# Out weights widened beside group 1, input weights during part 1's later stages, and four more raw buffers

## The chip, the cores and the metric

The kernel runs on one core of a Trainium2 chip. Its time is the device time of one execution, in microseconds (us). Three executions of the kernel before gave 655.83, 656.95 and 657.58, median 656.95.

## The reference, cut to what matters

```python
# attention over 2 x 8 heads, 768 positions, 64 columns a head: each query sees the keys less than
# 16 positions away, and one summary (maximum of keys, mean of values) per block of 32 keys
x = attention.transpose(0, 2, 1, 3).reshape(1536, 512)
xn = x / sqrt(mean(x * x) + 1e-6) * rms_g
g = xn @ w_gate; val = xn @ w_val                  # 512 x 1536 each       part 1
x = (g / (1 + exp(-g)) * val) @ w_out              # 1536 x 512
h = x @ w_in                                       # 512 x 2048            part 2
out = ((h - tanh(h)) @ w_out2)                     # 2048 x 512
```

The weights arrive as 64-bit floats. The result is float32.

## The kernel before, in words

**Numbers.** A float32 product is made of three matmuls (helper `mm3`, L807 to L809): each operand is split into a rounded high part and the rest, and high x high, low x high and high x low are added up. The high part is a ScalarE copy, the low part a subtraction on VectorE or GpSimd. A 64-bit weight must first become a float32: 128 x 512 of them are loaded as 512 KB into a raw buffer of 128 x 1024 words, ScalarE scales the upper words (L766, or L1278 for an out weight of part 2), VectorE shifts them (L767, L1279) and merges bits of the lower words (L768, L1280). The code calls this to widen. There are two raw buffers (pool `raw`), and a chain keeps their loads in one order on SyncE's queue.

**Stages.** Tokens go in three groups of four tiles of 128. Group 0's attention comes first. Beside its product with part 1's weights (`step`: w_gate and w_val in 12 blocks of 128 columns, then w_out) the attention of groups 1 and 2 runs (`one_unit`, 16 of the 24 units; the text calls this stage "beside group 1"). Then groups 1 and 2 go through part 1 together in six "wide" pairs of blocks (`combine`, `wide_pair`), with seven products instead of eight of sums and differences of sub-blocks; `combine` makes seven operands, each a high and a low part, of the tokens. Group 1's sum over w_out is made there. Group 2's is made in twelve late steps (`late_step`), one per block, 12 matmuls of 512 columns each: they read h from the weights' old places, round it (L825) and take the rest (L828). Part 2 then takes each group through eight pairs of blocks (`pair`), again with seven products per pair (42 matmuls of 256 columns) and 24 matmuls of 512 for the out weight; partial products are kept and added by L1425, L1444 and L1418, and L1479 and L1480 split the result.

**Part 2's weights.** For group 0 the input weights are widened (`widen_second`, 16 of them, one 512 KB load each), combined and split (`make`), and stored to DRAM tensors `ki`; groups 1 and 2 fetch them from there. Out weights are widened and split beforehand (`make_out`, 16 of them), stored as a high and a low half (`ko`, L1289), and fetched when used (L1257).

**Order.** The whole program is a list of operations with engine, estimated duration, dependences, buffers and a due time; `Plan.order` sorts it into one fixed order per engine before the program is built. Each engine then runs its order strictly, and an operation that waits holds up all behind it on its engine. A due time thus sets a place in the order. All DMAs stand on SyncE's queue.

**Places.** `hi_r`, `lo_r`, `wd_r`, `pad` and `rest` are regions of the on-chip memory which the stages use in turn. `pad` is the attention's workspace, `wd` holds part 1's weights, `hi_r[1]` and `hi_r[2]` are the high parts' places of groups 1 and 2. Before, `combine` put the operands 1 and 2 into `hi_r[1]` and `hi_r[2]`, and 6, 7, 5, 3 into `pad`, which is free after the last attention unit. `make_out` used places in `wd` that are free once the input weights of blocks 1 and 3 have been used (`gv_ops[1] + gv_ops[3]`), so all out weights came after group 0's steps.

## Time and profile before

| | us |
|---|---|
| median of three executions | 656.95 |
| profiled execution | 654.7 |
| its span, first to last instruction | 652.9 |
| TensorE busy | 634.8 |
| VectorE busy | 468.6 |
| ScalarE busy | 371.2 |
| GpSimd busy | 81.0 |

The page has the busy time of each engine, the span in 40 slices, the DMA queues, the chain of work that ended last, and the costliest groups of instructions. PE is TensorE, DVE VectorE, ACT ScalarE, POOL GpSimd, SP SyncE. Times in a timeline are from the start of the span. Matmuls overlap in the records (0.39 us each for 512 columns), so their rate is read from their starts. The stages in the span: group 0's attention to about 55 us, group 0's part 1 beside the other groups' attention to 197, the wide pairs to 350, the late steps to 385, part 2 to the end, with group 0 until 471.

### The profile page before, as it was taken

How to read it: one execution, taken by the hardware profiler on the slowest of the kernel's cores; microseconds unless marked ns; L12 is line 12 of the kernel's file. 1: busy time of each engine (PE TensorE's matmuls, PEld its weight loads, DVE VectorE, ACT ScalarE, POOL GpSimd, SP SyncE). 2: the span in 40 equal slices, each digit the busy share in tenths (PEclk: the TensorE clock that was granted, in tenths of full speed). 3: DMA queues.
4: the chain of work that ended last, by engine and by line, in shares of the span. 5: the costliest groups of instructions: out<-in, count | busy, mean ns of one | idle time of the engine just before them, and what ended most of it. 6: DMA issues, size and time to landing. Idle time of an engine off the chain costs nothing.

```text
span 652.9 us, 10519 instructions
## 1 busy us (share of the span) xinstructions
PE 634.8 (97%) x3642; PEld 542.3 (83%) x3642; DVE 468.6 (72%) x1037; ACT 371.2 (57%) x782; POOL 81.0 (12%) x142
## 2 busy tenths in 40 slices
PE   7999999999999999999999999989999999999996
PEld 6998888897888888888787878879989899888985
DVE  5789868886689799989988969986663343433333
ACT  3996676887665566666658747644553232433322
POOL 2213232131123024011200000010000000000000
PEclk9999999999999999999999999989999999999998
DMA  9987556555400023434452588977899787898742
GB/s 341 345 279 274 159 179 209 161 154 181 143 1 0 1 77 133 147 129 130 161 150 92 212 288 266 347 282 281 320 318 357 255 307 246 282 332 298 258 170 97
DMA packets 52254, 136.54 MB, mean 209 GB/s; under 512 B 6200, under 2 KB 8680, under 8 KB 52200
## 3 DMA queue, kind: packets, MB, share of 16 engines
q1 hardware_dynamic: 52200, 135.86, 61.1%
q8 instruction: 29, 0.48, 0.3%
q14 instruction: 25, 0.20, 0.1%
HBM read 109.62 MB, written 26.21 MB: 208 GB/s over the span
## 4 chain that ended last, share of the span: by engine, by line
PE 79%; DMA 10%; DVE 6%; ACT 3%; issue 1%; SPq 0%; POOL 0%; ACTq 0%; DVEq 0%; POOLq 0%
PE bank L809 14%; PE bank L807 14%; PE bank L808 14%; PE mid L807 10%; PE mid L809 9%; PE mid L808 9%; DMA raw<-in_w_dram 5%; PE bank L655 2%; PE bank L561 2%; DMA pad<-in_units_dram 2%; PE bank L666 1%; PE bank L612 1%; DMA out_dram<-th 1%; DMA wd<-in_ksum_dram 1%; DMA wd<-in_units_dram 1%
## 5 line engine op out<-in xcount | busy, mean ns | idle before, releaser
L809 PE MATMUL bank<-oh,hl 128*128 128x512 f32 x192 | 76.7, 399 | 0.9 <-DVE hl L1480 0.9
L807 PE MATMUL bank<-oh,hh 128*128 128x512 f32 x192 | 76.3, 398 | 0.1
L808 PE MATMUL bank<-ol,hh 128*128 128x512 f32 x192 | 75.5, 393 | 0.0
L1463 ACT ACTIVATE lo<-lo 128x512 f32<-128x512 f32 (+1 forms) x48 | 25.2, 524 | 57.4 <-DVE lo L1418 57.4
L807 PE MATMUL mid<-hi,ih 128*128 128x512 f32 (+1 forms) x136 | 54.0, 397 | 0.0
L807 PE MATMUL bank<-hh,oh 128*128 128x512 f32 (+1 forms) x128 | 50.2, 392 | 0.1
L809 PE MATMUL mid<-hi,il 128*128 128x512 f32 (+1 forms) x136 | 50.1, 368 | 0.0
L808 PE MATMUL bank<-hl,oh 128*128 128x512 f32 (+1 forms) x128 | 48.7, 380 | 1.0 <-DVE hl L828 0.8
L809 PE MATMUL bank<-hh,ol 128*128 128x512 f32 (+1 forms) x128 | 48.4, 378 | 0.0
L807 PE MATMUL mid<-pad,ih 128*128 128x512 f32 (+1 forms) x128 | 44.6, 349 | 2.1 <-ACT up L1425 1.9
L809 PEld LDWEIGHTS bank<-oh,hl 128*128 128x128 f32 x192 | 36.3, 189 | 10.5 <-DVE hl L1480 2.0
L1480 DVE TENSOR_TENSOR hl<-lo,hh 128x512 fp32r<-128x512 f32 x48 | 31.5, 687 | 18.2 <-ACT hh L1479 18.1
L808 PE MATMUL mid<-pad,ih 128*128 128x512 f32 (+1 forms) x128 | 44.4, 346 | 0.0
L809 PE MATMUL mid<-pad,il 128*128 128x512 f32 (+1 forms) x128 | 44.3, 346 | 0.0
L766 ACT ACTIVATE wd<-raw 128x512 f32<-128x512 f32 x46 | 31.0, 674 | 22.4 <-DMA raw<-in_w_dram 22.2
L1467 DVE TENSOR_TENSOR lo<-lo 128x512 f32<-128x512 f32 (+1 forms) x48 | 27.1, 565 | 22.9 <-ACT lo L1463 22.7
L808 PE MATMUL mid<-lo,ih 128*128 128x512 f32 (+1 forms) x112 | 40.6, 362 | 0.0
L807 PEld LDWEIGHTS bank<-oh,hh 128*128 128x128 f32 x192 | 36.4, 190 | 4.4 <-ACT hh L1479 0.3
L808 PEld LDWEIGHTS bank<-ol,hh 128*128 128x128 f32 x192 | 36.4, 190 | 4.5
L589 ACT ACTIVATE pad<-pad,st 128x184 f32<-128x184 f32 x88 | 32.3, 439 | 7.0 <-DVE st L575 7.0
L1418 DVE TENSOR_TENSOR lo<-up,bank 128x256 f32<-128x256 f32 x25 | 10.5, 419 | 36.0 <-PE bank L809 35.7
L1074 ACT COPY lo<-mid 128x512 f32<-128x512 f32 x36 | 21.1, 586 | 19.5 <-PE mid L809 19.1
(235 smaller groups left out, 1826.9 us busy)
## 6 DMA issues: line engine op xcount, KB each, us to landing
raw<-in_w_dram SPq DMA_DIRECT2D x62, 512.0 KB, 4.0
wd<-ki SPq DMA_DIRECT2D x32, 512.0 KB, 5.5
oh<-ko SPq DMA_DIRECT2D x48, 256.0 KB, 4.0
ol<-ko SPq DMA_DIRECT2D x48, 256.0 KB, 4.7
wd<-ki SPq DMA_DIRECT2D x32, 384.0 KB, 6.3
pad<-in_units_dram SPq DMA_DIRECT2D x19, 442.0 KB, 4.4
ko<-wd SPq DMA_DIRECT2D x32, 256.0 KB, 2.6
ki<-ih SPq DMA_DIRECT2D x7, 512.0 KB, 4.7
```

The costliest lines, as they stand in the source:

```text
L561: nc.tensor.matmul(ps[e][:, j * SC:(j + 1) * SC], q[r, j], k[r, j], start=(j == 0), stop=(j == NP - 1), skip_group_check=True,)
L589: nc.scalar.activation(s, s, AF.Exp, bias=st[:, 0, h:h + 1], scale=-1.0)
L655: nc.tensor.matmul(av[:, h * (D + 1):(h + 1) * (D + 1)], ph[:, h * P:(h + 1) * P], v[:, h], start=(h == 0), stop=False, skip_group_check=True,
L766: a = act(0.58, lambda d=d, w=w: nc.scalar.activation(d, w(k=1).bitcast(F32), AF.Prelu, scale=2.0 ** -112, alpha=-(2.0 ** 32)), ld, *after ...
L807: nc.tensor.matmul(o, ah, bh, start=first, stop=False, skip_group_check=True)
L808: nc.tensor.matmul(o, ah, bl, start=False, stop=False, skip_group_check=True)
L809: nc.tensor.matmul(o, al, bh, start=False, stop=last, skip_group_check=True)
L1074: o = act(0.52, lambda: nc.scalar.copy(u[m][:], mx[m][:]), *after, *wide_first, slots=[u[m], mx[m]])
L1418: return dve(0.38, lambda: nc.vector.tensor_tensor(out(), x(), z(), ALU.add), *after, slots=slots)
L1463: o = act(us, lambda: nc.scalar.activation(out(), x(), AF.Tanh), *after, slots=slots)
L1467: return dve(us, lambda: nc.vector.tensor_tensor(out(), x(), z(), ALU.subtract), *after, slots=slots)
L1480: l = dve(0.62, lambda j=j: nc.vector.tensor_tensor(hl[j][:], th[j][:], r32(hh[j][:]), ALU.subtract), h, slots=[th[j], hh[j], hl[j]], port ...
```

## The change

Six of the sixteen out weights (`SOON`) are now widened beside group 1, each with a due time before the end of that stage. Their results lie in `hi_r[1]` (pool `oq`, two places). For that `combine` has other homes: operands 1, 2, 6 and 7 in `pad`, 5 in `hi_r[2]`, 3 in `hi_r[1]`. The attention units of groups 1 and 2 are due 8 us sooner (`DONE`). The widening of part 1's weights from block 4 on, and the six out weights, alternate between the old raw buffers and two new ones in `hi_r[2]` (`rawt`); later every third load goes to one place in `wd` (`rawl`). The other ten out weights take turns in the list with the input weights, which go to other places (`AREA`: each pair of blocks of part 2 has its 1024 columns where a block of part 1's weights has been used up), and are made in one buffer (`op`) instead of three. `make_out` needs no separate place for the float32 value. A program that was built from each file gives the orders below. In the changed file L764 is L776, L766 is L778, L1276 is L1292, L1289 is L1306, L825 is L838, L783 is L796, L837 is L850, L1365 is L1381, L1425 is L1440, L1444 is L1459, L1463 is L1478 and L1479 is L1494.

```diff
 OPS = 7
 AHEAD = 20.0
+SOON = 6
 SLACK = 2.0
 BACK = 8
-DONE = 20.0
+DONE = 28.0
 LAND = 1.0
 FAR = 4.0
 GROWS = (slice(32, 64), slice(64, GROW + 2 * NB))
...
         h, f = divmod(f, NF1 // 2)
         return wd[h][:, f * W1:(f + 1) * W1]
+    AREA = 3, 7, 9, 11, 1, 6, 8, 10
+
     def w_second(f):
-        a = at_second(f)
-        return wd[1][:, a:a + 512]
-
-    def at_second(f):
-        n, e = divmod(f, 2)
-        if n < 6:
-            return ((2 * n + 1) if n < 3 else 2 * (n - 3)) * W1 + e * 512
-        return (2 * (n - 6) + e) * W1 + cut1
+        return area(f // 2)[:, f % 2 * 512:(f % 2 + 1) * 512]
+
+    def area(n):
+        h, a = divmod(AREA[n], NF1 // 2)
+        return wd[h][:, a * W1:a * W1 + 1024]
     def h_place(f):
         h, a = divmod(f, NF1 // 2)
...
     cut1 = 2 * NC_ * P
     chain = {}
-
-
+    as_u32 = lambda t: lambda: t().bitcast(U32)
+    plan.pools["rawt"] = Buffers([as_u32(hi_r[2].part(i * 1024, (i + 1) * 1024, F32)) for i in range(2)])
+    plan.pools["rawl"] = Buffers([wd[0][:, 5 * W1:5 * W1 + 1024].bitcast(U32)])
+    plan.pools["oq"] = Buffers([hi_r[1].part(i * 1024, (i + 1) * 1024, F32) for i in range(2)])
+    rawt_ops = []
+    rawl_ops = []
+    turn_raw = [0, 0]
+
+    def raw_slot(early):
+
+        turn_raw[early] += 1
+        n = turn_raw[early]
+        if early:
+            return (slot("rawt"), [], rawt_ops) if n % 2 else (slot("raw"), [], [])
+        return (slot("rawl"), gv_ops[5], rawl_ops) if not n % 3 else (slot("raw"), [], [])
     def widen(nm, src, dst, n, *after):
         done = []
...
                 raw = fixed(early_raw[i].bitcast(U32))
                 free = ksum_op[0] if i < 3 else vsum_op[0][0] + vsum_op[0][1]
             else:
-                raw = slot("raw")
-                free = []
+                raw, free, users = (slot("raw"), [], []) if nm in ("a0", "a1", "a2", "a3") else raw_slot(nm[0] == "a")
             d = dst[:, o:o + 512]
             du = d.bitcast(U32)
             w = lambda raw=raw, k=0: raw[:].rearrange("p (n k) -> p n k", k=2)[:, :, k]
...
     def combine(due):
         k2 = 1024
-        home = {1: (hi_r[1], 0), 2: (hi_r[2], 0), 4: (hi_r[0], 0)}
-        for i, n in enumerate((6, 7, 5, 3)):
+        home = {4: (hi_r[0], 0), 5: (hi_r[2], 0), 3: (hi_r[1], 0)}
+        for i, n in enumerate((1, 2, 6, 7)):
             home[n] = (pad, 2 * k2 * i)
         base = {(k, l): (lo_r[1 + l], k * k2) for k in range(2) for l in range(2)}
         base["t"] = (rest, 0)
...
         def split_sum(n, b, after, slots=()):
             r, a = home[n]
-            free = unit_ops if r is pad else first_ops if r is hi_r[0] else []
+            free = unit_ops if r is pad else {4: first_ops, 5: rawt_ops, 3: made_o}[n]
             by = due + 2 * MM * 2 * (1, 2, 6, 7, 5, 3, 4).index(n)
             out = []
             for c in range(2):
...
     for i, tag in enumerate(("lh", "ll")):
         plan.pools[tag] = Buffers([wd_r[0].part(k * 1024, (k + 1) * 1024, F32R) for k in range(i, 8, 2)])
     plan.pools["tb"] = Buffers([lo_r[0].part(i * 512, (i + 1) * 512, F32) for i in range(NC_)])
-    plan.pools["tq"] = Buffers([lo_r[2].part(i * 512, (i + 1) * 512, F32) for i in range(4)] + [lo_r[1].part(i * 512, (i + 1) * 512, F32) for i in range(2)])
+    plan.pools["tq"] = Buffers([lo_r[1].part(i * 512, (i + 1) * 512, F32) for i in range(2)] + [lo_r[2].part(i * 512, (i + 1) * 512, F32) for i in range(4)])
     plan.pools["sq"] = Buffers([rest.part(0, 1024, F32), lo_r[1].part(1024, 2048, F32)])
-    plan.pools["os"] = Buffers([wd[0][:, 3 * W1 + i * 512:3 * W1 + (i + 1) * 512] for i in range(2)])
-    plan.pools["op"] = Buffers([wd[0][:, W1:W1 + 1024]])
+    plan.pools["op"] = Buffers([area(4)])
     operand = {}
     ready = {}
     prepared = {}
...
     def make_out(f, due):
         n, j = divmod(f, 2)
-        raw, d, o = slot("raw"), slot("os"), slot("op")
+        early = f < SOON
+        raw, free, users = raw_slot(early)
+        o = slot("oq" if early else "op")
         w = lambda k: raw[:].rearrange("p (n k) -> p n k", k=2)[:, :, k]
-        du = lambda: d[:].bitcast(U32)
+        d = lambda: o[:, 512:]
+        du = lambda: d().bitcast(U32)
         src = w2[f].bitcast(U32)
-        gate = gv_ops[1] + gv_ops[3]
-        ld = dma(0.524, lambda: nc.sync.dma_start(raw[:], src[:, 1024:2048]), chain.get("raw"), slots=[raw], land=FAR)
+        gate = [] if early else gv_ops[1]
+        ld = dma(0.524, lambda: nc.sync.dma_start(raw[:], src[:, 1024:2048]), chain.get("raw"), *free, slots=[raw], land=FAR)
         chain["raw"] = ld
-        a = act(0.58, lambda: nc.scalar.activation(d[:], w(1).bitcast(F32), AF.Prelu, scale=2.0 ** -112, alpha=-(2.0 ** 32)), ld, *gate, slots=[raw, d])
-        a = dve(0.34, lambda: nc.vector.tensor_scalar(du(), du(), 3, None, ALU.logical_shift_left), a, slots=[d], port=True)
-        a = dve(0.6, lambda: nc.vector.scalar_tensor_tensor(du(), w(0), 29, du(), ALU.logical_shift_right, ALU.bitwise_or), a, slots=[raw, d], port=True)
-        a = act(0.52, lambda: nc.scalar.copy(o[:, :512].bitcast(F32R), d[:]), a, chain.get("op"), *gate, slots=[d, o])
+        a = act(0.58, lambda: nc.scalar.activation(d(), w(1).bitcast(F32), AF.Prelu, scale=2.0 ** -112, alpha=-(2.0 ** 32)), ld, *gate, slots=[raw, o])
+        a = dve(0.34, lambda: nc.vector.tensor_scalar(du(), du(), 3, None, ALU.logical_shift_left), a, slots=[o], port=True)
+        a = dve(0.6, lambda: nc.vector.scalar_tensor_tensor(du(), w(0), 29, du(), ALU.logical_shift_right, ALU.bitwise_or), a, slots=[raw, o], port=True)
+        users.append(a)
+        a = act(0.52, lambda: nc.scalar.copy(o[:, :512].bitcast(F32R), d()), a, chain.get("op"), slots=[o])
         chain["op"] = a
         def rest(on):
-            on.tensor_tensor(o[:, 512:].bitcast(F32R), d[:], o[:, :512], ALU.subtract)
-
-        z = flex({"pool": (1.32, lambda: rest(nc.gpsimd), True), "dve": (0.61, lambda: rest(nc.vector), True)}, a, slots=[d, o])
+            on.tensor_tensor(d().bitcast(F32R), d(), o[:, :512], ALU.subtract)
+
+        z = flex({"pool": (1.32, lambda: rest(nc.gpsimd), True), "dve": (0.61, lambda: rest(nc.vector), True)}, a, slots=[o])
         stored_o[f] = [
             dma(DM * P * 4e-6, lambda i=i: nc.sync.dma_start(r32(keep_o[n][j][i]), o[:, i * 512:(i + 1) * 512]), x, slots=[o], due=due, land=FAR)
             for i, x in enumerate((a, z))
...
         conv = [wide_op["b", f][0] for f in (f0, f1)]
         a11, a12 = d[0][:, 0:q], d[0][:, q:2 * q]
         a21, a22 = d[1][:, 0:q], d[1][:, q:2 * q]
-        a0, gap = at_second(f0), at_second(f1) - at_second(f0)
-        right = wd[1][:, a0:a0 + 2 * gap].rearrange("p (f c) -> p f c", f=2)[:, :, q:2 * q]
+        right = area(n).rearrange("p (f c) -> p f c", f=2)[:, :, q:2 * q]
         weights = {}
         store = []
         if n:
-            gate = gv_ops[5] + wide_ops
+            gate = gv_ops[5] + wide_ops + rawl_ops
             names = "ih", "il", "sm"
         else:
             gate = wide_ops + sq_ops
...
             for i, k in enumerate(ks):
                 weights[k] = (wh, wl, i * q, *done[i])
             at += m
-        if n:
-            after_a.extend([o1, o2, o3, o4] + [o for p in weights.values() for o in p[3:]])
+        after_a.extend([o1, o2, o3, o4] + [o for p in weights.values() for o in p[3:]])
         stored[n] = store
         return fetch_outs(n), weights
...
     for i in range(i0, 2 * NTILE):
         a, z = begin + LEAD, at - DONE
         unit(i // 2, i % 2, a + (z - a) * (i + 1 - i0) / (2 * NTILE - i0))
+    for i in range(SOON):
+        make_out(i, at - 4.0 * (SOON - i))
     combine(at - 2.0)
     wide = at
     for p in range(NF1 // 2):
...
     for k, f in enumerate(turn_f):
         late_step(k, f, at)
         at += 4 * MM
-    for i in range(10):
-        make_out(i, wide + (late - wide) * (i + 4) / 14)
     def widen_second(f):
-        n, e = divmod(f, 2)
-        if n < 3:
-            over = gv_ops[7 + 2 * n]
-        elif n < 6:
-            over = gv_ops[2 * n] + h_read[2 * n] + h_read[2 * n + 1]
-        else:
-            over = wo_ops[2 * (n - 6) + e + 6]
+        n = f // 2
+        a = AREA[n]
+        over = gv_ops[a]
+        if a % 2 == 0:
+            over = over + h_read[a] + h_read[a + 1]
+        if n == 4:
+            over = over + made_o
         wide_op["b", f] = widen(f"b{f}", w2[f].bitcast(U32), w_second(f), 512, *over)
-    for f in range(NF2):
-        widen_second(f)
-        if 10 + f < NF2:
-            make_out(10 + f, late + (at - late) * (f + 1) / 6)
+    for i in range(NF2 // 2):
+        for f in range(SOON + 2 * i, min(SOON + 2 * i + 2, NF2)):
+            make_out(f, wide + (late - wide) * (f + 1 - SOON + 2) / (NF2 - SOON + 2))
+        widen_second(2 * i)
+        widen_second(2 * i + 1)
     wo_last = [o for f in range(NF1) for o in wo_ops[f]]
     after_a = wo_last + [o for f in range(NF1) for o in h_read[f] + gv_ops[f]]
     for g in range(len(GROUPS)):
```

**ScalarE's order at the start of part 2.** The first copy of a partial product of part 2 is L1444 (L1459 in the changed file). Before, from the last rounding of h on:

```order
L825 CAST hh_104<-wd_0_67 128x512
L837 ACTIVATE lo_0_66<-mid_81 128x512
L837 ACTIVATE lo_0_66<-mid_82 128x512
L837 ACTIVATE lo_0_66<-bank_76 128x512
L766 ACTIVATE wd_0_68<-raw_89 128x512
L1278 ACTIVATE wd_0_67<-raw_90 128x512
L1444 COPY rest_71<-mid_81 128x256
```

Now, from the same place on:

```order
L838 CAST hh_104<-wd_0_67 128x512
L778 ACTIVATE wd_0_68<-raw_90 128x512
L1381 CAST ih_91<-wd_0_68 128x256
L850 ACTIVATE lo_0_66<-mid_81 128x512
L850 ACTIVATE lo_0_66<-mid_82 128x512
L1381 CAST ih_91<-wd_0_67 128x768
L778 ACTIVATE wd_0_68<-raw_89 128x512
L1381 CAST ih_92<-wd_0_68 128x512
L1459 COPY rest_71<-mid_81 128x256
```

Before, one input widening (L766, into `wd_0_68`) and one out weight (L1278) stand ahead of the copy; now there are two input widenings (L778), and three of the splits that make the first pairs' weights (L1381).

**ScalarE's order in the third and fourth pair of part 2.** Before, between one pair's splits (L1479) and the next pair's:

```order
L766 ACTIVATE wd_0_68<-raw_89 128x512
L1425 COPY rest_71<-mid_82 128x256
L1463 ACTIVATE lo_1_2038<-lo_1_2038 128x256
L1425 COPY lo_1_2038<-mid_82 128x256
L1365 CAST ih_91<-wd_0_68 128x256
L1365 CAST ih_91<-wd_0_67 128x768
L766 ACTIVATE wd_0_68<-raw_90 128x512
L1463 ACTIVATE lo_1_2038<-mid_82 128x256
L766 ACTIVATE wd_0_68<-raw_89 128x512
L1463 ACTIVATE lo_1_2038<-lo_1_2038 128x512
L1425 COPY up<-mid_81 128x256
L1479 CAST hh_103<-lo_1_2038 128x512
```

Now, in the same place:

```order
L1494 CAST hh_104<-lo_1_2089 128x512
L1440 COPY rest_71<-mid_82 128x256
L1478 ACTIVATE lo_1_2089<-lo_1_2089 128x256
L1440 COPY lo_1_2089<-mid_82 128x256
L1381 CAST ih_91<-wd_0_67 128x256
L1381 CAST ih_91<-wd_0_67 128x768
L1478 ACTIVATE lo_1_2089<-mid_82 128x256
L1381 CAST ih_92<-wd_0_67 128x512
L1381 CAST ih_92<-wd_0_67 128x256
L1478 ACTIVATE lo_1_2089<-lo_1_2089 128x512
L1440 COPY up<-mid_81 128x256
L1494 CAST hh_103<-lo_1_2089 128x512
```

Three input widenings with their loads are gone from it. In the changed file no L778 and no L1294 (L1278 before) stands behind the first L1459.

**SyncE's queue at the end of group 1's stage.** Before, the last loads of attention units (L520) and part 1's weights (L764) and the first out weights (L1276):

```order
L520 DMA pad_70<-in_units_dram 128x884
L764 DMA raw_89<-in_w_dram 128x1024
L764 DMA raw_90<-in_w_dram 128x1024
L520 DMA pad_70<-in_units_dram 128x884
L764 DMA raw_90<-in_w_dram 128x1024
L764 DMA raw_89<-in_w_dram 128x1024
L1276 DMA raw_90<-in_w_dram 128x1024
L1276 DMA raw_89<-in_w_dram 128x1024
L1276 DMA raw_90<-in_w_dram 128x1024
L1289 DMA ko_0_0_124<-wd_0_67 128x512
L1289 DMA ko_0_1_125<-wd_0_67 128x512
```

Now, around the last unit loads (L521):

```order
L776 DMA raw_89<-in_w_dram 128x1024
L1292 DMA hi_0_63<-in_w_dram 128x1024
L633 DMA pad_70<-in_tails_dram 30x260 x2
L521 DMA pad_70<-in_units_dram 128x884
L1292 DMA raw_90<-in_w_dram 128x1024
L1292 DMA hi_0_63<-in_w_dram 128x1024
L521 DMA pad_70<-in_units_dram 128x884
L633 DMA pad_70<-in_tails_dram 30x260 x2
L1292 DMA raw_89<-in_w_dram 128x1024
L1292 DMA hi_0_63<-in_w_dram 128x1024
L1306 DMA ko_0_0_124<-hi_0_62 128x512
L1306 DMA ko_0_1_125<-hi_0_62 128x512
```

Five of the six early out weights' loads (L1292), into `raw` and the new places in `hi`, stand there among the unit loads, and the first stores (L1306) come from `hi`.

## Rows read from the trace of the kernel before

**Rows 1.** The page, busy us (share of the span) and instructions by engine.

```profile
PE 634.8 (97%) x3642; PEld 542.3 (83%) x3642; DVE 468.6 (72%) x1037; ACT 371.2 (57%) x782; POOL 81.0 (12%) x142
```

**Rows 2.** Busy us (instructions) by stage; then granted clock, DMA share, GB/s.

```profile
60.00:190.00 130.00, 128.92 (x809) 107.61 (x809) 100.79 (x283) 94.02 (x207) 30.90 (x66) 1.00 0.51 156
190.00:350.00 160.00, 159.05 (x682) 127.68 (x681) 146.01 (x251) 97.64 (x179) 29.70 (x23) 1.00 0.31 99
350.00:385.00 35.00, 35.00 (x155) 28.97 (x156) 32.61 (x61) 24.40 (x47) 0.00 (x0) 1.00 0.58 199
385.00:445.00 60.00, 55.73 (x341) 48.94 (x340) 51.87 (x106) 36.22 (x78) 4.00 (x4) 0.97 0.85 298
```

**Rows 3.** Waits of ScalarE from 385 to 445: us in total, times, longest.

```profile
ACT wd L766 <- DMA raw<-in_w_dram: 8.5, 6, 2.5
```

**Rows 4.** Timeline of ScalarE: start, us, what, idle before and its releaser.

```profile
426.83 0.66 ACT L766 ACTIVATE wd<-raw 128x512 f32<-128x512 f32 x1 [2.50 <-DMA raw<-in_w_dram]
427.91 0.35 ACT L1425 COPY up<-mid 128x256 f32<-128x256 f32 x1
```

**Rows 5.** Timeline of TensorE in the first pairs of part 2.

```profile
389.22 0.39 PE L807 MATMUL mid<-pad,hi 128*128 128x256 f32 x1 [1.06 <-DVE rest L1418]
...
428.31 0.39 PE L807 MATMUL mid<-pad,ih 128*128 128x256 f32 x1 [1.36 <-ACT up L1425]
...
430.66 0.60 PE L809 MATMUL bank<-oh,hl 128*128 128x512 f32 x1 [0.49 <-DVE hl L1480]
...
433.61 0.41 PE L807 MATMUL bank<-pad,ih 128*128 128x256 f32 x1
```

**Rows 6.** The chain that ended last: two raw loads, start and duration.

```profile
380.53 6.09 DMA raw<-in_w_dram
...
420.97 5.83 DMA raw<-in_w_dram
```

**Rows 7.** The page, DMA issues: count, KB each, median us to landing.

```profile
raw<-in_w_dram SPq DMA_DIRECT2D x62, 512.0 KB, 4.0
```

**Rows 8.** Timeline of TensorE, equal points of four pairs of part 2.

```profile
406.78 0.39 PE L807 MATMUL bank<-oh,hh 128*128 128x512 f32 x1
...
417.29 0.39 PE L807 MATMUL bank<-oh,hh 128*128 128x512 f32 x1
...
443.10 0.39 PE L807 MATMUL bank<-oh,hh 128*128 128x512 f32 x1
```

**Rows 9.** Timelines of ScalarE and VectorE at the start of part 2.

```profile
386.65 0.66 ACT L766 ACTIVATE wd<-raw 128x512 f32<-128x512 f32 x1 [1.41 <-DMA raw<-in_w_dram]
...
387.35 0.43 DVE L767 TENSOR_SCALAR wd<-wd 128x512 uint32<-128x512 uint32 x1 [4.47 <-ACT wd L766]
```

**Rows 10.** Timelines of VectorE and TensorE in the last late step.

```profile
380.92 0.68 DVE L828 TENSOR_TENSOR hl<-wd,hh 128x512 fp32r<-128x512 f32 x1
...
382.40 0.39 PE L807 MATMUL mid<-hh,oh 128*128 128x512 f32 x1
...
385.13 0.28 PE L807 MATMUL mid<-pad,hi 128*128 128x256 f32 x1
```

**Rows 11.** Timeline of VectorE, three operations that follow each other.

```profile
372.35 0.41 DVE L767 TENSOR_SCALAR wd<-wd 128x512 uint32<-128x512 uint32 x1
372.69 0.68 DVE L828 TENSOR_TENSOR hl<-wd,hh 128x512 fp32r<-128x512 f32 x1
373.29 0.68 DVE L785 TENSOR_TENSOR ol<-wd,oh 128x512 fp32r<-128x512 f32 x1
```

**Rows 12.** Timelines of ScalarE and TensorE beside group 1.

```profile
151.72 0.66 ACT L766 ACTIVATE wd<-raw 128x512 f32<-128x512 f32 x1 [3.01 <-DMA raw<-in_w_dram]
...
154.81 1.44 PE L561 MATMUL bank<-pad 64*128 64x184 f32 x8 [1.04 <-POOL st L701]
```

**Rows 13.** Timeline of TensorE, attention's last turn and the first wide product.

```profile
184.81 0.60 PE L706 MATMUL bank<-ident,pad 128*128 128x128 f32 x4
...
197.04 0.40 PE L807 MATMUL mid<-hi,ih 128*128 128x512 f32 x1
```

More of the change, by code (lines that the diff above doesn't have):

```diff
@@ L282 @@
     psum = ctx.enter_context(tc.tile_pool(name="psum", bufs=1, space=bass.MemoryType.PSUM))
-    hi_r = [Region(const, f"hi{t}", NC_ * n * P, F32R) for t, n in GROUPS]
+    hi_r = [Region(const, f"hi{t}", NC_ * n * P, F32 if t else F32R) for t, n in GROUPS]
     lo_r = [Region(const, f"lo{t}", NC_ * n * P, F32 if t else F32R) for t, n in GROUPS]
@@ L897 @@
     ready_w = {}
-    wide_first = []
+    wide_free = []
     wide_all = []
@@ L962, in combine @@
         wide_all.extend(o for l in (s1, s2, t3, t1, t2, s6, s7, s5, s3, t4, s4) for c in l for o in c)
-        wide_first.extend(o for l in (s1, s2, t3, t1, t2, s6, s7, s5, s3, t4) for c in l for o in c)
+        flat = lambda *ls: [o for l in ls for c in l for o in c]
+        wide_free.extend((flat(s1, t1, t2, s6, t4), flat(t1, s5), flat(t3, s3)))
     wide_ops = []
@@ L1073, in keep @@
         def keep(m, u, *after):
-            o = act(0.52, lambda: nc.scalar.copy(u[m][:], mx[m][:]), *after, *wide_first, slots=[u[m], mx[m]])
-            return o
+            free = [] if p else wide_free[(ua, ub, uc).index(u)]
+            return act(0.52, lambda: nc.scalar.copy(u[m][:], mx[m][:]), *after, *free, slots=[u[m], mx[m]])
         def add(m, u, *after):
```

3 lines of the change are left out of this document (2 added, 1 removed).

## The prediction

> **What bounds the kernel now.** I read the page's busy shares first, then busy time by stage, then what the engines waited for, and last the timelines around those waits. TensorE is the bound: busy for 634.8 of 652.9 us, VectorE for 468.6 [rows 1]. By stage [rows 2] the reader is to see where it is not: beside group 1's attention (60 to 190 us) it idles 1.1 us, in part 1's wide products (190 to 350) 1.0, in the late steps (350 to 385) nothing, in the first pairs of part 2 (385 to 445) 4.3. In those first pairs the granted clock falls to 0.97 too. So what this change can win lies mostly in 60 us of the span, and the rest is a floor of matmuls which it does not touch.
>
> What ends the waits there: ScalarE itself waits 8.5 us, in six waits, for raw weight loads (L766) [rows 3]. The timelines show how that reaches TensorE. An L766 waits 2.50 us for its load and starts at 426.83, and L1425 stands behind it in ScalarE's order [rows 4]; TensorE, which needs that L1425, starts again at 428.31, 1.36 us late [rows 5]. The load had been issued at 420.97 and took 5.83 us [rows 6], against a median of 4.0 over all 62 [rows 7]. A second wait (0.49 us, for a low half) follows at 430.66, and then the clock drops: from there to 433.61 seven matmuls of 512 columns take 2.95 us, 0.42 each [rows 5], where twelve take 2.73 in a late step, 0.2275 each [rows 10].
>
> What that costs is read from equal points of the pairs [rows 8]: 406.78 to 417.29 is 10.51 us for one pair, and the two pairs from 417.29 to 443.10 take 25.81, which is 25.81 - 21.02 = 4.8 us too long. The two waits alone are 1.36 + 0.49 = 1.85 us. The Trainium skill (Perfetto Trace Analysis, Identifying the Most-Contended Engine) says that the busy share of matmuls is no good measure of TensorE's headroom. The trace agrees: by idle time this place would give back 1.85 us, by the starts 4.8, and I take the starts.
>
> **The change, part by part.** The sum is made against the profiled execution: 654.7 us, its span 652.9 and 1.8 around it. That is 2.25 below the median of 656.95, so I carry the difference over to the median.
>
> *A. The 4.8 us in the third and fourth pair of part 2.* Before, ten of part 2's sixteen input widenings stand on ScalarE behind the last half of the late steps, some in the place of the second order piece; now two are left there, both ahead of the first L1459 (L1444 before), and the pairs behind it hold none. Nothing in ScalarE's order then waits for a raw load, and the queue has eight loads of 512 KB less in the stretch. Next in line are the out weights' loads, for which TensorE never waited here. Bounds 0 and 4.8; I take 4.5, nearly all, since the rows show one cause for the first wait and the second follows it within 2.4 us.
>
> *B. The start of part 2.* The rest of the stage's idle time, 4.3 - 1.85 = 2.4 us, lies here, 1.06 of it in one wait [rows 5], again behind an L766, which starts at 386.65 for a load issued at 380.53; VectorE idles 4.47 us behind it [rows 6, 9]. Now an L778 (L766 before) for the very last load stands two rows ahead of that same copy, in the first order piece. Its buffer is freed by the widening before it, and the loads before it stand in one queue. One turn of a buffer costs 4.0 (load) + 0.66 (ScalarE) + 0.43 + 0.60 (VectorE) = 5.7 us at the median and 7.8 with a load of 6.1 [rows 6, 7, 9, 11]. About two turns follow between the ninth late step and the first additions, 11.4 to 15.6 us. TensorE's own work in between is three and a half late steps of 2.73 us [rows 10] and the 3.0 us from 385.13 to the wait that ended at 389.22 [rows 5, 10], 12.6 in all. So it may gain the 2.4 or lose up to 15.6 - 12.6 = 3.0 more. I take a gain of 0.5: a wait of another length in the same place.
>
> *C. The late steps.* VectorE is busy 32.6 of 35 us [rows 2]. Counted from the order between the first and the last low half of the late steps (0.60 us for 512 columns, 0.34 for 256 or for a shift, start to start [rows 11]), VectorE's work is 29.6 us before and 29.3 now: out-weight work leaves as input widening comes. So no change from the load on it. What is new is that six L778, not two, stand among ScalarE's rounded halves (L838, L825 before), of which two buffers exist. I take 0 and price the danger as a rival.
>
> *D. Beside group 1 (60 to 190).* Six out weights come here. Each is two ScalarE copies (0.66 at most each [rows 9]), three VectorE operations (0.34 + 0.60 + 0.60 [rows 11]), one load and two stores: 7.9 us of ScalarE and 9.2 of VectorE. ScalarE has 130 - 94.0 = 36.0 us free there and VectorE 29.2, and the DMA share is 0.51 [rows 2], so all of it fits. In return four raw buffers serve the first part's widening, not two: ScalarE's wait of 3.01 us for a load, behind which TensorE idled 1.04 [rows 12], should go. The attention units are to end 8 us sooner (DONE 28, not 20), with the same matmuls. Bounds: 1.0 gained, 9.2 lost if nothing of VectorE's work were hidden. I take 0, as the free time is three times what comes.
>
> *E. The start of the wide products.* Operands 1 and 2 now lie in the attention's workspace and wait for its last unit. Before, 197.04 - 184.81 = 12.2 us lay between the attention's last turn and the first wide product [rows 13]. In the new order 75 matmuls of 512 columns stand there, 75 x 0.2275 = 17.1 us. What must fit in is ScalarE's copy and four casts (5 x 0.66) and eight VectorE operations of 0.60, 8.1 us. Covered, so 0; without the cover each us of it would be one of TensorE's.
>
> *F. Inside the wide products.* VectorE is the tight one, 146.0 of 160 us [rows 2]. Over wide and late steps out weights fall from 15 to 10 (5 x 1.54 = 7.7 us of VectorE) and input widenings rise from 6 to 14 (8 x 0.94 = 7.5 us), while GpSimd leaves three subtractions of 512 columns and three of 256 to VectorE and takes two of 512 from it (3 x 0.60 + 3 x 0.34 - 2 x 0.60 = 1.6 us). Net about +1.4 us where it idles 14.0. Bounds 1.0 gained (TensorE's idle time there) and 1.4 lost; I take 0.
>
> Sum: 4.5 + 0.5 = 5.0 us gained: 654.7 - 5.0 = 649.7 for the profiled execution, 656.95 - 5.0 = **652.0 us** for the median.
>
> **The rivals.** *1. All goes well:* no wait is left at the start of part 2 (2.4), beside group 1 (1.0) and in the wide products (1.0), and A gives 4.8: 9.2 us, 647.8. For it: these waits have the same kind of cause. Against it: the two turns of a buffer at B.
>
> *2. The waits only move:* A is won, but B costs its 3.0, and a drop of the clock comes with it, 2.95 - 7 x 0.2275 = 1.4 us as after 430.66 [rows 5, 10]. 4.5 - 3.0 - 1.4 = 0.1: 656.9. For it: the same kind of instruction stands ahead of the same copy.
>
> *3. The late steps stall (slower):* ScalarE's order is the place. Between the ninth and the eleventh late step the load of input weight 11 has 1.5 steps, 4.1 us, and a low half now ends 0.8 us before TensorE needs it (380.92 + 0.68 against 382.40 [rows 10]). It decides at a load of 4.9 us. At the 6.1 of [rows 6] the loads of weights 11, 12 and 13 cost 1.2 us each, 3.6; with B at its worst (3.0) and one clock drop (1.4) that is 8.0 against A's 4.5: 3.5 slower, 660.5. For it: loads, stores and products share the queue there. Against it: the median load is 4.0, and three buffers serve. The Trainium skill (DMA: Bandwidth & Descriptors, Latency and other measured facts) says that HBM's access time grows under load; the loads of 5.83 and 6.09 us beside other transfers agree, without showing the cause.
>
> *4. Group 1 pays:* if half of D's 9.2 us were not hidden, 4.6 of the 5.0 are gone: 656.6. Against it: the free time there.
>
> **How the numbers follow.** The forecast has 0.47, rival 1 0.17, rival 2 0.13, rival 4 0.08, rival 3 0.15. A measurement of this kernel can tell about 0.3%, 2.0 us, from no change, so faster means below 655.0. Forecast and rival 1 are faster but for 0.03, rivals 2 and 4 no change but for 0.01 that ends slower: faster 0.61, same 0.23, slower 0.16. The range reaches from a little past rival 1, whose parts were each taken whole, to the middle of rival 3's way: 647.0 to 659.0; the likeliest case's own is 649.5 to 654.5.
>
> **What would show it.** Right: the two pairs in place of the 25.81 us take 21.0 to 21.3; no L778 in ScalarE's order past the first L1459; a granted clock of 1.00 after 400 us; TensorE's idle time from 385 to 445 falls from 4.3 to about 2. For rival 3: waits of TensorE for L841 (L828 before) between 350 and 385. For rival 4: idle time between 60 and 190 well above 1.1 us. For E: a wait of the first wide product for L946 (L933 before). The prediction is wrong if the time to part 2's first product grows by over 2 us, or if pairs after the first still wait for ScalarE.

## The result and the profile after

Six executions of the changed kernel have a median of 650.78 us (650.23 to 652.61); the kernel before, six on the same chip, 657.01 (655.83 to 657.58). The ratio is 0.9911, 95% interval 0.9895 to 0.9926: some 5.8 us faster. Forecast were 652.0, range 647 to 659. The profiled execution took 651.4, its span is 649.6.

First the page of the changed kernel: busy shares, and the line of the raw loads (count, KB each, median us from issue to landing).

```profile
PE 633.4 (98%) x3642; PEld 541.1 (83%) x3642; DVE 470.1 (72%) x1039; ACT 372.1 (57%) x782; POOL 76.0 (12%) x140
...
raw<-in_w_dram SPq DMA_DIRECT2D x39, 512.0 KB, 5.1
```

TensorE's count is the same and it bounds as before [rows 1]; the raw loads that go to the old places land later than before (median 5.1 against 4.0, [rows 7]). Then its busy time by stage, columns as in [rows 2].

```profile
60.00:190.00 130.00, 127.32 (x794) 104.78 (x791) 109.43 (x301) 98.12 (x217) 35.54 (x69) 1.00 0.61 200
190.00:350.00 160.00, 160.00 (x688) 128.90 (x686) 142.69 (x250) 96.76 (x175) 21.73 (x18) 1.00 0.27 86
350.00:385.00 35.00, 34.31 (x152) 28.30 (x152) 33.00 (x60) 24.24 (x45) 0.00 (x0) 1.00 0.55 169
385.00:445.00 60.00, 57.73 (x368) 51.72 (x367) 48.55 (x98) 35.98 (x78) 5.66 (x7) 1.00 0.71 255
```

From 385 to 445 us TensorE's idle time fell from 4.3 to 2.3 us, the clock stayed at full speed, and the DMA share is lower. Beside group 1 the idle time rose, from 1.1 to 2.7. TensorE's waits in the first pairs, and the one of ScalarE for a raw load there (engine, tile, line, releaser: us, times, longest):

```profile
PE mid L820 <- DVE rest L1433: 1.2, 1, 1.2
PE mid L820 <- ACT rest L1440: 0.5, 1, 0.5
PE bank L820 <- DVE lo L1433: 0.4, 1, 0.4
PE mid L820 <- ACT lo L850: 0.2, 1, 0.2
...
ACT wd L778 <- DMA raw<-in_w_dram: 2.6, 1, 2.6
```

ScalarE's six waits for raw loads (8.5 us, [rows 3]) are one of 2.6, at the start of part 2. TensorE's timeline at that start and at the points of [rows 8]:

```profile
386.47 0.39 PE L820 MATMUL mid<-pad,hi 128*128 128x256 f32 x1 [0.22 <-ACT lo L850]
...
390.81 0.39 PE L820 MATMUL mid<-pad,hi 128*128 128x256 f32 x1 [1.20 <-DVE rest L1433]
...
418.53 0.39 PE L820 MATMUL bank<-oh,hh 128*128 128x512 f32 x1
...
439.55 0.39 PE L820 MATMUL bank<-oh,hh 128*128 128x512 f32 x1
```

Against the trace of before, part 2's first product comes 1.3 us later (386.47 for 385.13), and so does the point before the two slow pairs (418.53 for 417.29); behind them it is 3.55 sooner (439.55 for 443.10). The two pairs take 21.02 us, not 25.81. So the profiled executions differ by 3.3 us, all of it won in these two pairs; the rest of the 6 us of the medians is not in this pair of traces. Where it lies, a second trace of the kernel before was to show.

### The profile page after: what moved, and what is told of

It is laid out like the page before. It is cut to its first block, busy times and chain, and to the rows that moved or that the text cites. A ratio compares the mean times of both kernels' runs of the same rounds, so it can differ in the third digit from the quotient of the medians.

```text
span 649.6 us, 10543 instructions
## 1 busy us (share of the span) xinstructions
PE 633.4 (98%) x3642; PEld 541.1 (83%) x3642; DVE 470.1 (72%) x1039; ACT 372.1 (57%) x782; POOL 76.0 (12%) x140
## 4 chain that ended last, share of the span: by engine, by line
PE 85%; DVE 5%; DMA 4%; ACT 4%; issue 1%; SPq 0%; POOL 0%; ACTq 0%; DVEq 0%
PE bank L820 15%; PE bank L822 15%; PE bank L821 15%; PE mid L820 10%; PE mid L822 10%; PE mid L821 10%; PE bank L656 3%; PE bank L562 2%; PE bank L667 1%; DMA out_dram<-th 1%; PE bank L613 1%; ACT pad L590 1%; DMA raw<-in_w_dram 1%; DMA wd<-in_ksum_dram 1%; DMA pad<-in_tails_dram 1%
## 5 line engine op out<-in xcount | busy, mean ns | idle before, releaser
L820 PE MATMUL mid<-hi,ih 128*128 128x512 f32 (+1 forms) x160 | 63.6, 397 | 0.0
L822 PE MATMUL mid<-hi,il 128*128 128x512 f32 (+1 forms) x160 | 59.6, 373 | 0.0
L1478 ACT ACTIVATE lo<-lo 128x512 f32<-128x512 f32 (+1 forms) x48 | 25.2, 525 | 58.3 <-DVE lo L1433 58.3
L1433 DVE TENSOR_TENSOR lo<-up,bank 128x256 f32<-128x256 f32 x25 | 10.5, 419 | 35.7 <-PE bank L822 35.6
L820 PEld LDWEIGHTS mid<-hi,ih 128*128 128x128 f32 x160 | 30.1, 188 | 6.6 <-issue 2.3
L820 PE MATMUL mid<-pad,ih 128*128 128x256 f32 (+1 forms) x104 | 35.0, 337 | 0.5 <-ACT rest L1440 0.5
L822 PEld LDWEIGHTS mid<-hi,il 128*128 128x128 f32 x160 | 30.1, 188 | 5.7
L821 PE MATMUL mid<-pad,ih 128*128 128x256 f32 (+1 forms) x104 | 34.8, 335 | 0.0
L822 PE MATMUL mid<-pad,il 128*128 128x256 f32 (+1 forms) x104 | 34.7, 334 | 0.0
```

The lines of the kernel that those rows point to most:

```text
L820: nc.tensor.matmul(o, ah, bh, start=first, stop=False, skip_group_check=True)
L821: nc.tensor.matmul(o, ah, bl, start=False, stop=False, skip_group_check=True)
L822: nc.tensor.matmul(o, al, bh, start=False, stop=last, skip_group_check=True)
L1433: return dve(0.38, lambda: nc.vector.tensor_tensor(out(), x(), z(), ALU.add), *after, slots=slots)
L1478: o = act(us, lambda: nc.scalar.activation(out(), x(), AF.Tanh), *after, slots=slots)
```

## The experiments

Ratios are to the kernel before on the same chip, 95% interval in brackets. "First product" and the columns right of it say how much later (+) or sooner (-) than in the first trace of before a matmul of part 2 starts: its first product (385.13 there), the point at 406.78, the end of the two pairs (443.10), the last product (646.74). In the four kernels whose matmuls stand in another order there (old places, no early out weights, early raw buffers alone, before with part 2's loads planned longer) it is the matmul before which as many columns have been done. The row of the run without early out weights is that of its second try.

| run | ratio | first product | 406.78 | 443.10 | last |
|---|---|---|---|---|---|
| changed kernel | 0.9911 (0.9895 to 0.9926) | +1.3 | +1.3 | -3.6 | -3.3 |
| before, again | one execution, 657.11 us | +0.9 | +2.4 | +2.4 | +2.4 |
| no third late buffer | 0.9918 (0.9888 to 0.9949) | -1.7 | +1.2 | -3.2 | -2.6 |
| that, and old places | 0.9971 (0.9953 to 0.9988) | +0.4 | +0.1 | -1.5 | -0.9 |
| attention due 20 ahead | 0.9964 (0.9939 to 0.9988) | +2.9 | +2.8 | -2.0 | -1.4 |
| no early raw buffers | 1.0054 (1.0032 to 1.0075) | +8.9 | +8.7 | +3.9 | +3.9 |
| no early out weights | 1.0152 (1.0111 to 1.0193) | +6.6 | +5.8 | +14.9 | +14.8 |
| early raw buffers alone | 1.0188 (1.0163 to 1.0213) | +3.0 | +5.3 | +11.4 | +11.7 |
| changed, part 2's loads planned longer | 0.9892 (0.9850 to 0.9933) | -0.6 | -0.8 | -5.6 | -5.1 |
| that, part 1's too | 1.0051 (1.0030 to 1.0072) | +6.3 | +6.1 | +1.3 | +1.5 |
| that for part 2, attention due 32 ahead | 1.0022 (1.0003 to 1.0040) | +5.5 | +5.2 | +0.4 | +0.8 |
| before, part 2's loads planned longer | 0.9911 (0.9894 to 0.9928) | -1.8 | -3.2 | -5.7 | -3.0 |

**The kernel before, again** (no edit).

> The kernel before, unchanged, for a second trace. Its profiled execution was 2.3 us shorter than its median (654.7 against 656.95), while the changed kernel's was 0.6 us longer than its own. Theory: the two waits in the third and fourth pair of part 2 depend on when raw loads land, so in most executions this place loses more than the 4.8 us of the first trace; in this run the two pairs take 26 to 29 us in place of 25.81 and the time is 655.8 to 657.6. Rival: the two pairs take 25.8 again and the rest lies elsewhere.

The two pairs take 445.53 - 419.81 = 25.72 us, as in the first trace (25.81), with the same kind of cause: ScalarE waits 9.6 us for raw loads in seven waits. So the theory fell, and the rival held. What is new is 1.6 us between 390 and 396, after waits for L1418 of 1.05 and 0.41 us; the first trace has nearly the same two (1.06 and 0.41) and loses nothing behind them. TensorE's waits and its busy row from 385 to 445 in this run:

```profile
PE mid L807 <- ACT up L1425: 1.5, 1, 1.5
PE mid L807 <- DVE rest L1418: 1.0, 1, 1.0
PE mid L807 <- ACT rest L1425: 0.8, 1, 0.8
...
PE bank L807 <- DVE lo L1418: 0.4, 1, 0.4
...
385.00:445.00 60.00, 55.47 (x332) 48.94 (x331) 49.97 (x101) 36.22 (x77) 3.99 (x4) 0.94 0.83 286
```

From 392.01 to 394.79 matmuls of 256 columns follow each other after 0.21 us, not 0.12: the granted clock, 0.94 over the stretch, fell here to the lower of its levels too, as it does at 430 in both traces. The second of the two waits in the first trace, then in this one with what follows:

```profile
390.61 0.39 PE L807 MATMUL bank<-pad,hi 128*128 128x256 f32 x1 [0.41 <-DVE lo L1418]
```

```profile
391.47 0.39 PE L807 MATMUL bank<-pad,hi 128*128 128x256 f32 x1 [0.41 <-DVE lo L1418]
...
392.01 0.42 PE L807 MATMUL bank<-pad,hi 128*128 128x256 f32 x1
...
394.79 0.41 PE L808 MATMUL mid<-pad,ih 128*128 128x256 f32 x1
```

Against this trace the changed kernel is 5.7 us sooner at the end: 4.7 of it in the two pairs and 1.7 from the first product to 396, with 0.5 lost ahead of these and 0.3 behind.

**No third late raw buffer.**

```diff
-return (slot("rawl"), gv_ops[5], rawl_ops) if not n % 3 else (slot("raw"), [], [])
+return slot("raw"), [], []
```

> The changed kernel without the third raw buffer of the later stages; the early ones stay. In the new order four L778 stand behind the first L1459 on ScalarE, none in the changed kernel. Theory (raw loads that ScalarE waits for among the pairs of part 2 cost TensorE): 1 to 3 us slower than the changed kernel, 651.8 to 653.8, and a wait of ScalarE for a raw load after 390 us. Rival (the places alone matter, a third buffer does nothing): 650.8.

No difference is shown: the ratio is that of the changed kernel within its interval, which reaches to 0.9949. As the theory has it ScalarE waits more for raw loads in the pairs (7.5 us, longest 4.5), and TensorE loses 1.16 + 1.72 = 2.9 us between its first product and 406.78. But from 347 to the first product it wins 1.3 us against before, where the changed kernel wins nothing: no low half is late at 350. In these two traces the third buffer thus costs ahead of the pairs part of what it wins in the first of them.

**The same, with part 2's input weights in their old places.** On the run above, `at_second`, `w_second`, `right` and `widen_second` have their old bodies:

```diff
-over = gv_ops[a]
...
+if n < 3:
+    over = gv_ops[7 + 2 * n]
+elif n < 6:
+    over = gv_ops[2 * n] + h_read[2 * n] + h_read[2 * n + 1]
+else:
+    over = wo_ops[2 * (n - 6) + e + 6]
```

> As the run without the third late raw buffer, and part 2's input weights back in the places of the kernel before; six early out weights and early raw buffers stay. Eight L778 stand behind the first L1459. Theory: all of the gain in the pairs is lost, 4.5 us: about 655.3, and the two pairs in which the kernel before took 25.81 us take over 24. Rival (the third buffer was the cure): no slower than the run that lacks only that buffer. Rival (the six out weights out of the way are the cure): 650.8.

Two thirds of the gain are gone: ratio 0.9971 against 0.9918. Eight L778 (L785 here) stand behind the first copy, and in the pairs ScalarE waits 9.7 us for raw loads. The two pairs take 23.0 us, not over 24 as the theory has it. So the new places bring some 3.5 us, and the rest of the change without them and the third buffer some 2.

**No early out weights**, twice. The first try:

```diff
-SOON = 6
+SOON = 0
...
-for f in range(SOON + 2 * i, min(SOON + 2 * i + 2, NF2)):
+for f in range(SOON + 4 * i, min(SOON + 4 * i + 4, NF2)):
```

> The changed kernel without early out weights: all sixteen are made in the later stages, four ahead of each of the first four input weights' pairs. Ten L778 then stand behind the first L1459. Group 1 has its old load on ScalarE and VectorE again. Theory: TensorE's idle time from 60 to 190 us falls from 2.7 back to about 1 and the first product of part 2 comes 1.3 to 2 us sooner, but 4.5 us are lost in part 2's first pairs: 653.5 to 654.5. Rival (early out weights cost group 1 nothing): 655.3. Rival (they are not needed): 649.

696.39 us, ratio 1.0646, for a reason that is none of the theories'. One wait of TensorE from 385 to 445:

```profile
PE mid L820 <- ACT ih L1381: 29.0, 1, 29.0
```

The second pair's sums lie where the third late buffer is, and are gated by all its users (`rawl_ops`), which now stood far behind. The edit made a wait of its own and says nothing on out weights. The second try has no third buffer, three out weights per step, and the out weights' place last in `AREA` (their buffer `op`, and the input weights that wait for it, move along: `area(7)`, `n == 7`):

```diff
-SOON = 6
+SOON = 0
...
-AREA = 3, 7, 9, 11, 1, 6, 8, 10
+AREA = 3, 7, 9, 11, 6, 8, 10, 1
...
-return (slot("rawl"), gv_ops[5], rawl_ops) if not n % 3 else (slot("raw"), [], [])
+return slot("raw"), [], []
...
-for f in range(SOON + 2 * i, min(SOON + 2 * i + 2, NF2)):
+for f in range(3 * i, min(3 * i + 3, NF2)):
```

> No early out weights and no third late raw buffer, the new places kept (the one that the out weights use now comes last), three out weights ahead of each of the first input weights' pairs. Eight L778 and three out weights stand behind the first L1459. It replaces the run without early out weights in which the pairs' sums waited for the third buffer. Theory: the new places alone do not clear the pairs, the early out weights do: 653 to 656, at least 2 us slower than the run that lacks only the third buffer (650.8), which has four L778 there. Rival (places are enough): 650.8. Rival (out weights in group 1 cost TensorE time): below 650.

667.16 us: 1.5% slower than the kernel before. It loses 6.6 us up to part 2, 2.0 of it in a wait at the start of the wide products, and 9 from 406.78 to the end of the two pairs, where TensorE waits up to 3.1 us for ScalarE's casts. So without the early out weights the rest of the change is slower than the kernel before, with the new places here, and with the old ones in the run with the early raw buffers alone, below.

**Attention due 20 us ahead.**

```diff
-DONE = 28.0
+DONE = 20.0
```

> The changed kernel with attention due 20 us before the wide products, as before, not 28. Theory (VectorE has free time beside group 1 either way, and the start of the wide products is covered): within 1 us of the changed kernel, 650 to 652, with no wait for L946 or L945's copies at the start of the wide products. Rival (the earlier due is needed since operands 1 and 2 lie in the workspace): a wait of 1 us or more there, 652 or more. Rival (the denser attention costs group 1 its 1.7 us of waits): 649.

The first rival holds: 3.5 us slower than the changed kernel by the ratios, and the place is the one named: the wide products' start. It is not L946 that TensorE waits for but L1040 behind it, 2.1 us in two waits.

**No early raw buffers:**

```diff
-return (slot("rawt"), [], rawt_ops) if n % 2 else (slot("raw"), [], [])
+return slot("raw"), [], []
```

> The changed kernel without the two extra early raw buffers: part 1's widening and the six early out weights share two buffers. Theory (my step on group 1: two buffers make ScalarE wait for loads, which cost TensorE 1.04 us before; six more loads in the same stretch add to it): 1 to 2 us slower, 652 to 653, waits of ScalarE for raw loads from 60 to 190 us of over 11 us in all. Rival (loads are never last there): 650.8.

9 us slower than the changed kernel, and not where it was looked for. ScalarE waits 12.9 us for raw loads beside group 1, yet TensorE loses nothing there (idle 1.1); from 190 to 225 it waits:

```profile
PE mid L820 <- ACT ih L1037: 3.7, 1, 3.7
PE mid L822 <- POOL il L1040: 1.6, 1, 1.6
```

and the clock falls behind them (0.97 from 190 to 350). Both runs point at VectorE's row L946, six casts in one block that make the operands in `hi_r`. Its start in the changed kernel, with attention due 20 ahead, in the later run due 32 ahead, and in the second try without early out weights:

```profile
199.59 3.69 DVE L946 TENSOR_TENSOR hi<-lo,hi 128x512 fp32r<-128x512 f32 x6
```

```profile
200.44 3.70 DVE L946 TENSOR_TENSOR hi<-lo,hi 128x512 fp32r<-128x512 f32 x6
```

```profile
202.71 3.69 DVE L946 TENSOR_TENSOR hi<-lo,hi 128x512 fp32r<-128x512 f32 x6
```

```profile
202.17 3.70 DVE L946 TENSOR_TENSOR hi<-lo,hi 128x512 fp32r<-128x512 f32 x6
```

The first wide product starts at 198.76, 197.85, 197.54 and 200.24 us in these traces, so L946 starts 0.8, 2.6, 5.2 and 1.9 us behind it. At 0.8 (three more runs with the same order have 0.8 too) TensorE does not wait; at 1.9 it waits 2.0 us, at 2.6 2.1, at 5.2 3.9. By these the wide products' start has at most some 1.1 us of slack in the changed kernel, if L946 alone sets it; the waits do not grow in step with it, so other rows ahead of L1040 count too.

**Part 2's raw loads planned to land 4.0 us after issue**, not 1.0, in `widen`:

```diff
-ld = dma(0.524, ..., chain.get("raw"), *free, slots=[raw])
+ld = dma(0.524, ..., chain.get("raw"), *free, slots=[raw], land=FAR if nm[0] == "b" else LAND)
```

> The changed kernel with one number for its planner: part 2's input weights are planned to land 4.0 us after their issue, not 1.0 (their loads took 5 to 6 us in the trace), which puts the sums of the first pair ahead of some of the last casts and two L778 behind the first L1459. Theory (the 1.36 us wait at the start of part 2 comes from VectorE rows that stand ahead of L1433 because loads are planned too short): 1 us faster, 649.8. Rival (the two L778 that it moves behind the first L1459 make ScalarE wait there): no change or up to 1.5 us slower.

649.87 us; its ratio's interval overlaps the changed kernel's, so 0.9 us is not shown. The wait that the theory means is one of 1.20 us (1.36 is the wait for L1425 in the trace of before). In the trace it is gone, but smaller ones (0.5, 0.5, 0.4, 0.4) stand in its place: from first product to 406.78 it wins 0.2 where the changed kernel wins 0.1.

**The same for part 1's loads, and attention due 32 ahead**, each an edit on the run above:

```diff
-land=FAR if nm[0] == "b" else LAND)
+land=FAR)
```

```diff
-DONE = 28.0
+DONE = 32.0
```

> The run with the longer planned landing, for part 1's input weights too (all raw loads planned at 4.0 us). Theory (the planner's order follows the loads better wherever it knows their time): 0 to 1.5 us faster than with part 2's alone, 648.4 to 649.9, idle time of TensorE from 60 to 190 us below 1.5. Rival (part 1's rows now come late for group 1 or for the wide products' start, where VectorE has no slack): 651 or more, with a wait at the wide products' start.

> The run with the longer planned landing of part 2's weights, and attention due 32 us before the wide products, not 28. Theory (VectorE has no slack left at the wide products' start, 20 us cost 3.9): nothing waits there at 28, so no more is to be had: 649.4 to 650.4. Rival (a shorter margin still costs at 28): 648.5 to 649. Rival (denser attention costs group 1): 651 or more, idle time from 60 to 190 us above 2.5.

The first went as its rival has it: TensorE waits 4.1 us for L1037 and L1040, though beside group 1 its idle time is 0.2, as the theory says. The second fits none of its theories: idle time beside group 1 is 1.9, and yet the wide products' start, which a longer margin was to help, waits 3.9 us. L946 starts at 202.71, and VectorE had waited 5.7 us for ScalarE's copies in the early out weights (in the changed kernel 1.5). Its waits from 150 to 205:

```profile
DVE hi L1302 <- ACT hi L1298: 3.1, 3, 1.5
DVE hi L1295 <- ACT hi L1294: 2.6, 2, 2.1
```

All waits of VectorE in that stretch add up to 8.3 us, though, against 7.9 in the changed kernel, so these are not shown to be the cause. The due time moved the planner's order as well.

**The early raw buffers alone**, with the new homes of the wide operands: no third buffer, old places, and

```diff
-SOON = 6
+SOON = 0
-DONE = 28.0
+DONE = 20.0
-for i in range(NF2 // 2):
...
+for i in range(10):
+    make_out(i, wide + (late - wide) * (i + 4) / 14)
+for f in range(NF2):
+    widen_second(f)
+    if 10 + f < NF2:
+        make_out(10 + f, late + (at - late) * (f + 1) / 6)
```

> The two extra early raw buffers and the new homes of the wide operands alone: no early out weights, part 2's weights in the old places and in the old order of widening, attention due 20 us ahead, no third late buffer. Theory (each of the other parts is needed too): no faster than the kernel before, 655 to 658, with ten L778 behind the first L1459 and waits of ScalarE for raw loads among the pairs. Rival (the early raw buffers alone bring the gain): 651 to 653.

12 us slower than the kernel before, with nearly the same work behind the first L1459 (ten L778 and an out weight, nine there). TensorE waits 2.2 us at the wide products' start, and ScalarE 12.7 us for raw loads from 385 to 500. The waits of TensorE from 385 to 500 us (here L1389 is L1381, L1448 is L1440):

```profile
PE mid L827 <- ACT ih L1389: 3.4, 1, 3.4
PE mid L827 <- ACT rest L1448: 2.3, 1, 2.3
PE mid L827 <- ACT up L1448: 1.2, 1, 1.2
```

**The kernel before, with part 2's loads planned longer**: the same edit as above, on the old file, and nothing of the change.

> The kernel before with one number for its planner, as in the run of the changed kernel with the longer landing: part 2's input weights planned to land 4.0 us after their issue, not 1.0. Places, buffers and out weights as before; ten L766 stand behind the first L1444. Theory (the pairs of part 2 need the input weights widened earlier, and no order of the same work behind the late steps does it): 654 to 657, idle time of TensorE from 385 to 445 us still over 3.5. Rival (the kernel before only suffers from loads planned too short, and the places and buffers of the change are not what helps): 650 to 653.

The rival holds for the time: 649.93 us, ratio 0.9911, what the whole change brings. Ten L766 stand behind the first L1444 (nine before). But ScalarE hardly waits for their loads; its wait for raw loads, and the busy row, from 385 to 445:

```profile
ACT wd L766 <- DMA raw<-in_w_dram: 1.3, 1, 1.3
...
385.00:445.00 60.00, 57.29 (x359) 50.48 (x357) 50.07 (x103) 38.05 (x80) 8.32 (x6) 1.00 0.85 300
```

8.5 us in six waits became 1.3 in one, the clock stays up, and idle time falls from 4.3 to 2.7 with the same DMA load (share 0.85). So ScalarE standing at widenings before their loads had landed was a cost. But the two pairs, with four widenings left among them, still take 23.4 us, not 21.0. The longest wait of TensorE there, and the one of ScalarE ahead of it, which is for a store that frees its buffer:

```profile
433.53 0.93 ACT L1365 CAST ih<-wd 128x512 fp32r<-128x512 f32 x2 [2.62 <-DMA ki<-ih]
```

```profile
435.87 0.39 PE L807 MATMUL mid<-pad,ih 128*128 128x256 f32 x1 [1.15 <-ACT up L1425]
```

Nor does the gain lie where the change has it: of the 3.0 us at the end of this trace 1.8 are won ahead of part 2's first product, where no low half is late at 350, and 3.9 from there to the end of the two pairs; behind it 2.7 are lost again, 2.0 of them in waits for L1368 and L1480. (The trace is of an execution 1.7 us above this run's median.)

## Why the prediction was right, step by step

*A (4.5 taken, bound 4.8): right, and the whole of it.* The two pairs won 25.81 - 21.02 = 4.79 us. All four signs came: no L778 behind the first L1459, 21.0 us for the pairs, a clock of 1.00, idle time 2.3. The Trainium skill (Perfetto Trace Analysis, Identifying the Most-Contended Engine) says that the busy share of matmuls is no good measure of how close TensorE is to its limit. The trace agrees, since idle time would have given 1.85 us here; the page gives pipelining as the reason, and here part of the rest is the lower clock (1.4 us behind 430.66). The cause is shown from both sides: in all eight kernels in which no widening of an input weight stands in the two pairs they take 21.0 us; in the others 23.0 (old places), 23.4 (before, loads planned longer), 25.7 and 25.8 (before) and over 29 (the two slowest). Of the 4.8 us in the kernel before the waits for raw loads are by this about half: without them, with four widenings left in the two pairs, these take 23.4. What I implied besides, that the waits go because no widening is left there, is one of two ways; for the pairs it is the better one. One sign of being wrong came in small: a pair after the first still waits for ScalarE, the second, 0.46 us for L1440 at 397.41 (before 0.58 and 0.17 there).

*B (0.5 taken): 0.1 in the first pair of traces*, +1.3 at both ends, with a wait of 1.20 us for the same addition (L1433, L1418 before) in place of 1.06: the wait stayed, as the step said, but another row ends it. The L778 two rows ahead of the copy L1459 found its load landed (ScalarE's 2.6 us lie at the widening before it), the copy was done at 389.31, and the addition stood behind low parts (L1384) on VectorE:

```profile
387.87 0.67 ACT L778 ACTIVATE wd<-raw 128x512 f32<-128x512 f32 x1
...
388.94 0.37 ACT L1459 COPY rest<-mid 128x256 f32<-128x256 f32 x1
```

```profile
389.20 1.22 DVE L1384 TENSOR_TENSOR il<-wd,ih 128x512 fp32r<-128x512 f32 x1
390.35 0.41 DVE L1433 TENSOR_TENSOR rest<-rest,mid 128x256 f32<-128x256 f32 x1
```

Against the second trace of before it is 1.7, because there the clock fell behind that wait. This was priced only as a loss (rival 2's 1.4 us), not as one that the kernel before may itself pay. The sum was made on the first trace, and against that the changed kernel's trace wins 3.3 us, not the 5.0 of the forecast. That 652.0 lies so near to 650.78 is in part luck: other executions of the kernel before, as the second trace, pay more than the one that was read.

*C, F (0): right.* TensorE idles nowhere from 190 to 350, and 0.7 us at 350 for L841 (before 0.65 for L828, at the same matmul). F's count of VectorE did not come: from 190 to 385 it was busy 175.7 us, against 178.6 before, where I had expected 1.4 more.

*D (0): right, though its trace first seemed to speak for rival 4.* Idle time rose from 1.1 to 2.7 us, and the first product of part 2 came 1.3 late. But three runs carry out the same orders on all engines up to the wide products' start, and there idle time is 1.2, 1.2 and 1.5. One point of TensorE in the changed kernel's trace (125.18, behind a wait for L576), and in two of them:

```profile
125.18 1.11 PE L656 MATMUL bank<-pad 128*128 128x65 f32 x8 [1.04 <-DVE st L576]
```

```profile
123.57 1.00 PE L656 MATMUL bank<-pad 128*128 128x65 f32 x8
```

```profile
123.64 1.00 PE L656 MATMUL bank<-pad 128*128 128x65 f32 x8
```

Counted at the first wide product, the changed kernel's trace is 1.7 us later than the first trace of before, the three runs 0.9 and 0.3 later and 0.1 sooner, and the second trace of before 0.9 later. So executions of one order differ there by up to 1.8 us, and of the early out weights' 9.2 us of VectorE no cost beyond that is seen, as taken. Where D failed is the price of the new buffers. I put the early ones at up to 1.0 us of gain, from a wait beside group 1; without them the kernel loses 9, at the wide products' start.

*E (0, "covered"): the number was right, the reason not.* I counted 17.1 us of matmuls between the attention's last turn and the first wide product as cover. The first wide product does not wait in any run; the next ones do, for L1037 and L1040, behind L946 on VectorE. That queue has some 1 us of slack, and I did not look at it. Seven of the runs wait there, 2.0 to 5.3 us.

*The rivals.* Rival 1's full 9.2 us did not come, the waits of rival 2 moved only at B, the late steps of rival 3 held, rival 4 was one execution. A rival that I lacked would have been the largest: that the change's parts are worth something only together, since the planner's order shifts with each. Alone or with one missing they range from 12 us slower than before (with the edit that made its own wait left out) to as fast as the whole.

Open: why planning part 1's loads longer, or attention due 32 ahead, delays L946 was not traced further, and whether the changed kernel with part 2's loads planned longer is really faster than it (0.9892 against 0.9911) needs more runs. No run beat the changed kernel measurably.

## What to carry to other kernels

Where a planner orders the work, its constants are part of the kernel: before places and buffers are moved to relieve a wait, compare the planned time of the transfer with the landing in the trace. Here one number, 1.0 us planned against 4 to 6 in the rows, gave as much time as the whole change. It is no rule that a number nearer to the rows is better everywhere: the same 4.0 us for part 1's loads as well took the changed kernel from a ratio of 0.9892 to 1.0051. Count a stall from equal points, with what the clock does behind it, and take a second trace of the kernel before you explain a difference of a few us. A new order is tested whole: its parts alone can cost more than it gains.

## What the runs showed of the hardware

A wait of TensorE of some 1 to 2 us may cost more than itself: behind it the clock fell to its lower level for about 3 us in both traces of before (at 430), in the second also at 392, and after 3.7 us of waiting in the run without early raw buffers (0.97 from 190 to 350); behind the changed kernel's wait of 1.20 us it did not. Nearly the same two waits (1.06 and 0.41 us, 1.05 and 0.41) went either way in two executions of one kernel, and made 1.6 of the 2.4 us by which these differ. Raw loads to the old places took 5.1 us at the median in the changed kernel and 4.0 before, and yet ScalarE waited less for them (2.6 us, not 8.5, from 385 to 445): a later landing costs nothing where nothing stands waiting for it.
